# Opening loads in partition halves, 512-byte weight rows, and other operands for the warm-up matmuls in a fused state-space and gated-MLP kernel

## The chip, the cores and the metric

The kernel runs on one core of one Trainium2 chip. The metric is the device time of one execution in microseconds (us). The kernel before takes 214.58 us in the median of 4 runs (214.56 to 214.65).

## What is computed

The input x has 2048 rows of 512 values in bfloat16. It is normalised row by row, and three terms are added: x itself, a diagonal state-space layer and a gated MLP with 1792 hidden columns. Cut to what matters:

```python
xn = (x - mean(x)) / sqrt(var(x) + 1e-5)          # per row of 512
# A: h[t] = Lam_bar * h[t-1] + B_bar @ xn[t]  (512 complex states, 2048 steps)
#    yA[t] = 2 * Re(C @ h[t]) + Dskip * xn[t]
# B: yB = (silu(xn @ w1) * (xn @ w3)) @ w2         # w1, w3: 512 x 1792, w2: 1792 x 512
out = x + yA + yB
```

## The kernel before

The 2048 rows are cut into 4 blocks of 512 rows, and each block into 4 chunks of 128 rows (one row on each of the 128 partitions). The 1792 hidden columns are 14 tiles of 128 (f = 0 to 13). The engines' orders are written out by hand: an instruction goes to its engine's queue in the order in which the Python code emits it, and a small list of background tasks (`Filler`) puts VectorE work between the matmul groups.

For block 0 the start is special, and it is what the change touches.

- **Loads (L136 to L143).** The four row chunks of block 0 are loaded by one DMA each, chunks 0 and 2 from SyncE's queue (SP), chunks 1 and 3 from ScalarE's queue (ACT). Then come the gate weights: `load_w(a, b)` loads columns a to b of w1 from one queue and of w3 from the other. First f = 0 alone (rows of 256 bytes), then f = 1 and 2 (rows of 512 bytes). GpSimd's queue (POOL) loads three small parameter rows.
- **`bulk_loads` (L144 to L155).** A one-column VectorE copy into `w1_sb` (L145), which reads the statistics of chunk 1, stands ahead of it; the next load overwrites that column, so SP has to wait for the copy. Then SP issues the weights of f = 3 to 7, the next block of x, the transposing loads of B and C, the other weights.
- **Warm-up (L162 to L170).** VectorE fills a tile `warm` with zeros, and `keep_busy(9, 512)` runs nine matmuls of 512 columns on it, whose result is not used.
- **Normalisation of a chunk.** `ln_stats` (L189, L190) gives mean and variance on VectorE, `ln_first_rstd` (L203, L204) gives 1/sqrt by a logarithm and an exponential on ScalarE, `ln_apply` (L194) normalises on VectorE. `ln_first_transpose` turns the chunk by four TensorE transposes into PSUM (L209), called T0 to T3 below, and a ScalarE copy (L210) brings it to `xnT`. The pool of these PSUM tiles (`ps_y`) has two buffers, and the warm-up's output tile holds one of them.
- **Quarters (L466 to L469).** `quarter(cl, f)` multiplies chunk cl with the w1 and the w3 tile of f: 8 matmuls of 128 columns at L442. There are 12 of them, q(0,0) to q(3,2). The six PSUM tiles that they fill are then evacuated by ScalarE (L451 with Silu, L452), after `preload_act_table_set("silu_and_others")` at L500.
- From f = 3 on, block 0 goes on with matmuls of 512 columns at L442, then the state-space input (`bu`, L370), the rest of f, and the other blocks; y is formed at L546 and L552, and L557 and L558 finish and store it.

The order on TensorE at the start is: nine dummies, T0, 8 dummies of 128 columns, T1, q(0,0), q(1,0), T2, a small transpose of the parameters (L270), q(0,1), q(0,2), q(1,1), q(1,2), T3, then the six quarters of chunks 2 and 3, then f = 3.

Of the kernel before, what the change touches and what calls it, by code (L numbers as in the profile page):

```python
# [12 lines left out]
ACT = mybir.ActivationFunctionType  # L13

FP32 = DT.float32
BF16 = DT.bfloat16
P = 128
# [34 lines left out]
def kernel(  # L52
# [17 lines left out]
    nc = tc.nc  # L70
# [3 lines left out]
    CPB = 4  # L74
    TBLK = CPB * P
# [6 lines left out]
    FIRST = 3  # L82
    MID = 8
# [3 lines left out]
    xv = A_x[0].rearrange("(c p) d -> p c d", p=P)  # L87
# [3 lines left out]
    const = ctx.enter_context(tc.tile_pool(name="const", bufs=1))  # L91
# [13 lines left out]
    w1_sb = const.tile([P, NDT, F], BF16, name="w1_sb")  # L105
# [23 lines left out]
    def load_w(f0, f1, eng1=nc.sync, eng3=nc.sync):  # L129
        eng1.dma_start(out=w1_sb[:, :, f0:f1], in_=w1v[:, :, f0:f1])  # L130
        eng3.dma_start(out=w3_sb[:, :, f0:f1], in_=w3v[:, :, f0:f1])
# [1 line left out]
    def load_x(b):  # L133
        nc.sync.dma_start(out=x_blk[b], in_=xv[:, b * CPB:(b + 1) * CPB, :])

    for c in range(CPB):  # L136
        eng = nc.sync if c % 2 == 0 else nc.scalar
        eng.dma_start(out=x_blk[0][:, c, :], in_=xv[:, c, :])
    load_w(0, P, nc.sync, nc.scalar)
    load_w(P, FIRST * P, nc.sync, nc.scalar)  # L140
    for i, src in enumerate((A_log_dt, A_Lambda_re, A_Lambda_im)):
        nc.gpsimd.dma_start(out=par_rows[i * NPT:(i + 1) * NPT, :], in_=src.rearrange("(t p) -> t p", p=P))

    def bulk_loads():  # L144
        nc.vector.tensor_copy(out=w1_sb[:, 0, FIRST * P:FIRST * P + 1], in_=mv_all[:, 1, 0:1])  # L145
        load_w(FIRST * P, MID * P)
        load_x(1)
        nc.sync.dma_start_transpose(out=bt_re, in_=A_B_re)
        nc.sync.dma_start_transpose(out=bt_im, in_=A_B_im)
        load_w(MID * P, 11 * P)  # L150
        load_w(11 * P, F)
        nc.sync.dma_start_transpose(out=ct_re, in_=A_C_re)
        nc.sync.dma_start_transpose(out=ct_im, in_=A_C_im)
        nc.sync.dma_start(out=w2_sb, in_=B_w2.rearrange("(t p) d -> p t d", p=P))
        nc.sync.dma_start(out=dskip_row, in_=A_Dskip.partition_broadcast(P))  # L155
# [3 lines left out]
        load_x(3)  # L159


    warm = const.tile([P, TBLK], BF16, name="warm")  # L162
    nc.vector.memset(warm, 0.0)
    wps = ps_y.tile([P, TBLK], FP32, name="y_ps")

    def keep_busy(n, cols):
        for _ in range(n):
            nc.tensor.matmul(out=wps[:, 0:cols], lhsT=warm[:, 0:P], rhs=warm[:, 0:cols], start=True, stop=True)

    keep_busy(NWARM, TBLK)  # L170
    nc.scalar.preload_act_table_set("natural_log_exp_and_others")
# [15 lines left out]
    def ln_stats(b, cl):  # L187
        stats = lnp.tile([P, 6], FP32, name="stats", bufs=4)
        nc.vector.bn_stats(out=stats, in_=x_blk[b][:, cl, :])  # L189
        nc.vector.bn_aggr(out=mv_all[:, b * CPB + cl, :], in_=stats)  # L190

    def ln_apply(b, cl):
        c = b * CPB + cl
        nc.vector.tensor_scalar(out=xn_blk[b][:, cl, :], in0=x_blk[b][:, cl, :], scalar1=mv_all[:, c, 0:1],  # L194
                                scalar2=rstd_all[:, c:c + 1], op0=ALU.subtract, op1=ALU.mult)
# [5 lines left out]
    def ln_first_rstd(cl):  # L201
        lnv = lnp.tile([P, 1], FP32, name="lnv")
        nc.scalar.activation(out=lnv, in_=mv_all[:, cl, 1:2], func=ACT.Ln, bias=eps_t, scale=1.0)  # L203
        nc.scalar.activation(out=rstd_all[:, cl:cl + 1], in_=lnv, func=ACT.Exp, scale=-0.5)  # L204

    def ln_first_transpose(cl):
        pxt = ps_y.tile([P, NDT, P], BF16, name="y_ps")
        for dt in range(NDT):
            nc.tensor.transpose(out=pxt[:, dt, :], in_=xn_blk[0][:, cl, dt * P:(dt + 1) * P], identity=ident)  # L209
        return lambda: nc.scalar.activation(out=xnT_blk[0][:, :, cl * P:(cl + 1) * P], in_=pxt, func=ACT.Copy)  # L210
# [47 lines left out]
    kr = const.tile([P, NPT], FP32, name="kr")  # L258
# [16 lines left out]
        nc.scalar.activation(out=dtv, in_=par[:, 0:NPT], func=ACT.Exp)  # L275
        gp.tensor_tensor(out=kr, in0=dtv, in1=lre, op=ALU.mult)

    def params_rho():
        nc.scalar.activation(out=rho, in_=kr, func=ACT.Exp)
        gp.tensor_tensor(out=turn, in0=dtv, in1=lim, op=ALU.mult)  # L280
        gp.tensor_scalar(out=turn, in0=turn, scalar1=1.0 / TWO_PI, scalar2=None, op0=ALU.mult)
        gp.tensor_scalar(out=fr, in0=turn, scalar1=MAGIC, scalar2=None, op0=ALU.add)
        gp.tensor_scalar(out=fr, in0=fr, scalar1=-MAGIC, scalar2=None, op0=ALU.add)
        gp.tensor_tensor(out=fr, in0=turn, in1=fr, op=ALU.subtract)
        gp.tensor_scalar(out=t0, in0=turn, scalar1=0.25, scalar2=None, op0=ALU.add)
        gp.tensor_scalar(out=ab, in0=t0, scalar1=MAGIC, scalar2=None, op0=ALU.add)
        gp.tensor_scalar(out=ab, in0=ab, scalar1=-MAGIC, scalar2=None, op0=ALU.add)
        gp.tensor_tensor(out=ab, in0=t0, in1=ab, op=ALU.subtract)
        gp.tensor_tensor(out=den, in0=lre, in1=lre, op=ALU.mult)
        gp.tensor_tensor(out=t0, in0=lim, in1=lim, op=ALU.mult)  # L290
        gp.tensor_tensor(out=den, in0=den, in1=t0, op=ALU.add)
# [143 lines left out]
    def glu(b):  # L435
        hg_blk[b] = hgp.tile([P, NFT, TBLK], BF16, name="hgT")
        xnT, hgT = xnT_blk[b], hg_blk[b]
        pend = []

        def mms(ps, w, f, tsl):  # L440
            for dt in range(NDT):
                nc.tensor.matmul(out=ps[:, tsl], lhsT=w[:, dt, f * P:(f + 1) * P], rhs=xnT[:, dt, tsl],  # L442
                                 start=(dt == 0), stop=(dt == NDT - 1))

        pair = []

        def evac(f, g_ps, u_ps):
            if f % 2 == 0:
                pair[:] = [glup.tile([P, 2, TBLK], BF16, name="g16"), glup.tile([P, 2, TBLK], BF16, name="u16")]
            g16, u16 = pair  # L450
            nc.scalar.activation(out=g16[:, f % 2, :], in_=g_ps, func=ACT.Silu)  # L451
            nc.scalar.activation(out=u16[:, f % 2, :], in_=u_ps, func=ACT.Copy)  # L452
            if f % 2 == 1:
                pend.append((f, g16, u16))

        def gate():
            f, g16, u16 = pend.pop(0)
            nc.vector.tensor_tensor(out=hgT[:, f - 1:f + 1, :], in0=g16, in1=u16, op=ALU.mult)  # L458

        f0 = 0  # L460
        if b == 0:
            f0 = FIRST
            tiles = [(ps_gu if i < 4 else ps_bu).tile([P, TBLK], FP32, name="gu_ps" if i < 4 else "bu_ps")
                     for i in range(2 * FIRST)]

            def quarter(cl, f):  # L466
                tsl = slice(cl * P, (cl + 1) * P)
                mms(tiles[2 * f], w1_sb, f, tsl)
                mms(tiles[2 * f + 1], w3_sb, f, tsl)  # L469

            ln_stats(0, 0)
            ln_first_rstd(0)
            ln_stats(0, 1)
            ln_first_rstd(1)
            bulk_loads()
            ln_apply(0, 0)
            ln_first_transpose(0)()
            keep_busy(8, P)
            ln_stats(0, 2)
            ln_first_rstd(2)  # L480
            ln_apply(0, 1)
            ln_first_transpose(1)()
            quarter(0, 0)
            ln_stats(0, 3)
            ln_first_rstd(3)
            ln_apply(0, 2)
            ln_apply(0, 3)
            quarter(1, 0)
            ln_first_transpose(2)()
            pps = params_transpose()  # L490
            params_dt(pps)
            params_rho()
            table_angles(0)
            table_angles(1)
            for f in (1, 2):
                quarter(0, f)
            for f in (1, 2):
                quarter(1, f)
            ln_first_transpose(3)()
            nc.scalar.preload_act_table_set("silu_and_others")  # L500
            for cl in (2, 3):
                for f in range(FIRST):
                    quarter(cl, f)
            evac(0, tiles[0], tiles[1])
            evac(1, tiles[2], tiles[3])
            evac(2, tiles[4], tiles[5])
            gate()
            bg.fill(2.0)
        for f in range(f0, NFT):
            if b == 0 and f == MID:  # L510
                ssm_tasks(0)
                bu(0)
            g_ps = ps_gu.tile([P, TBLK], FP32, name="gu_ps")
            mms(g_ps, w1_sb, f, slice(0, TBLK))
            u_ps = ps_gu.tile([P, TBLK], FP32, name="gu_ps")
            mms(u_ps, w3_sb, f, slice(0, TBLK))
            evac(f, g_ps, u_ps)
            if b == 0 and f == FIRST:
                sin_step((0, 0))
            elif b > 0 or f != MID - 1:  # L520
                sin_step()
            bg.fill(1.35)
            if pend and f % 2 == 0:
                gate()
        return gate
# [132 lines left out]
```

## Time and profile before

| what | value |
|---|---|
| median of 4 runs | 214.58 us |
| the profiled execution's own time | 214.56 us |
| its span, from first to last instruction | 212.5 us |
| TensorE matmuls busy | 206.9 us (97% of the span) |
| VectorE busy | 155.7 us (73%) |
| ScalarE busy | 116.4 us (55%) |
| GpSimd busy | 24.7 us (12%) |
| first row chunk on its way (DMA, from 0.73 us) | 2.82 us |
| first transposes on TensorE | at 5.84 us |
| first quarter on TensorE | at 7.23 us |
| first matmul of f = 3 | at 13.73 us |
| last DMA issue | at 209.77 us |

How to read it: PE is TensorE's matmuls, PEld its weight loads, DVE is VectorE, ACT ScalarE, POOL GpSimd, SP SyncE. A q behind a name (SPq, ACTq) is that engine's queue issuing a DMA. All times are microseconds from the first instruction. 2.06 us of the execution's own time lie outside the span. A line such as `xn<-x_blk` names the tile written and the tile read; `x4` is the number of instructions merged; what stands in square brackets is the engine's idle time before and what ended it.

### The profile page before, as it was taken

What the parts mean: (1) busy time and instruction counts of PE and PEld (TensorE: products, weight loads), DVE (VectorE), ACT (ScalarE), POOL (GpSimd) and SP (SyncE); (2) the same over time, 40 slices, a digit from 0 to 9 for tenths busy, and PEclk for the clock granted to TensorE, in tenths of its full rate; (3) what the DMA queues carried; (4) which work ended last, traced back from release to release, by engine and by line L of the source; (5) the groups of instructions that cost most, each with busy time, mean ns of one, the idle gap of its engine ahead of it and who ended that gap; (6) DMA issues with size and microseconds to landing.
All of it is one profiled execution on the core that took longest, in us unless ns stands there. A gap on an engine that the chain in (4) does not pass through costs nothing.

```text
span 212.5 us, 2774 instructions
## 1 busy us (share of the span) xinstructions
PE 206.9 (97%) x1056; PEld 98.7 (46%) x1056; DVE 155.7 (73%) x186; ACT 116.4 (55%) x219; POOL 24.7 (12%) x50
## 2 busy tenths in 40 slices
PE   7899999999999999999999999999999999999993
PEld 2774444444444444444444444444444444444463
DVE  3599799999937969899999897828999981121111
ACT  3689897699866864066666786036667620000000
POOL 7170279300000030000000012000000000000000
PEclk9999999999999999999999999999999999999999
DMA  4999999700000003500000001510000000100100
GB/s 139 336 245 261 252 282 222 222 0 0 3 0 0 0 0 77 96 27 0 0 0 5 0 0 25 123 52 0 2 0 0 3 0 2 48 25 29 48 25 26
DMA packets 26797, 13.68 MB, mean 64 GB/s; under 512 B 16544, under 2 KB 26784, under 8 KB 26784
## 3 DMA queue, kind: packets, MB, share of 16 engines
q1 hardware_dynamic: 25200, 12.78, 25.0%
q10 hardware_dynamic: 1488, 0.72, 1.2%
q8 instruction: 8, 0.13, 0.3%
q14 instruction: 5, 0.04, 0.1%
q0 software_dynamic: 96, 0.00, 0.0%
HBM read 7.74 MB, written 2.10 MB: 46 GB/s over the span
## 4 chain that ended last, share of the span: by engine, by line
PE 94%; ACT 1%; DMA 1%; DVE 1%; issue 0%
PE gu_ps L442 45%; PE y_ps L546 23%; PE y_ps L552 13%; PE bu_ps L370 12%; DMA x_blk<-in_A_x_dram 1%; PE bu_ps L442 1%; PE y_ps L209 1%; DVE stats L189 1%; ACT xnT L210 1%; ACT u L372 1%; ACT tabe L337 0%; DVE o L557 0%; DVE mv_all L190 0%; DVE xn L194 0%; DVE w_sb L145 0%
## 5 line engine op out<-in xcount | busy, mean ns | idle before, releaser
L442 PE MATMUL gu_ps<-xnT,w_sb 128*128 128x512 bf16 (+1 forms) x488 | 96.7, 358 | 0.2 <-ACT xnT L210 0.2
L442 PEld LDWEIGHTS <-w_sb 128*128 128x128 bf16 x520 | 46.9, 98 | 50.3 <-issue 0.4
L546 PE MATMUL y_ps<-w_sb,hgT 128*128 128x512 bf16 (+1 forms) x238 | 50.2, 366 | 0.0
L452 ACT ACTIVATE u<-gu_ps 128x512 bf16<-128x512 f32 x55 | 33.3, 606 | 11.4 <-PE gu_ps L442 10.8
L451 ACT ACTIVATE g<-gu_ps 128x512 bf16<-128x512 f32 x55 | 33.2, 603 | 9.4 <-PE gu_ps L442 9.4
L557 DVE TENSOR_TENSOR o<-y_ps,xn 128x512 bf16<-128x512 f32 (+1 forms) x17 | 11.2, 657 | 36.0 <-PE y_ps L552 36.0
L546 PEld LDWEIGHTS <-hgT 128*128 128x128 bf16 x238 | 23.3, 98 | 25.3
L372 ACT ACTIVATE u<-bu_ps 128x512 bf16<-128x512 f32 x32 | 19.1, 597 | 24.2 <-PE bu_ps L370 24.2
L406 DVE TENSOR_TENSOR_SCAN u<-rho,h,u 128x512 bf16<-128x512 f32 x24 | 29.5, 1270 | 0.2
L458 DVE TENSOR_TENSOR hgT<-g,u 128x1024 bf16<-128x1024 bf16 x28 | 19.0, 682 | 5.7 <-ACT u L452 5.7
L552 PEld LDWEIGHTS <-h 128*128 128x128 bf16 x136 | 13.3, 98 | 14.3
L552 PE MATMUL y_ps<-ct_re,h 128*128 128x512 bf16 (+1 forms) x68 | 16.6, 366 | 0.0
L552 PE MATMUL y_ps<-ct_im,h 128*128 128x512 bf16 (+1 forms) x68 | 16.6, 366 | 0.0
L370 PE MATMUL bu_ps<-xnT,bt_re 128*128 128x512 bf16 x64 | 16.4, 379 | 0.1
L370 PE MATMUL bu_ps<-xnT,bt_im 128*128 128x512 bf16 x64 | 16.4, 379 | 0.0
L393 DVE TENSOR_TENSOR p<-u,tabe 128x2048 bf16<-128x2048 bf16 x8 | 9.8, 1221 | 3.5 <-ACT u L372 3.4
L242 POOL TENSOR_SCALAR acc<-acc 128x4 f32<-128x4 f32 x2 | 1.0, 500 | 80.1 <-ACT xn L241 80.1
L411 DVE TENSOR_TENSOR p<-u,tabe 128x2048 bf16<-128x2048 bf16 x8 | 9.8, 1223 | 0.2
L418 DVE TENSOR_TENSOR h<-h,p 128x2048 bf16<-128x2048 bf16 x8 | 9.8, 1223 | 0.2
L396 DVE TENSOR_TENSOR u<-u,tabe 128x2048 bf16<-128x2048 bf16 x8 | 9.8, 1223 | 0.2
L400 DVE TENSOR_TENSOR u<-u,p 128x2048 bf16<-128x2048 bf16 x8 | 9.8, 1225 | 0.1
L370 PEld LDWEIGHTS <-bt_re 128*128 128x128 bf16 x64 | 6.2, 98 | 7.8 <-issue 0.3
(91 smaller groups left out, 137.1 us busy)
## 6 DMA issues: line engine op xcount, KB each, us to landing
out_dram<-o SPq DMA_DIRECT2D x15, 128.0 KB, 1.7
w_sb<-in_B_w_dram SPq DMA_DIRECT2D x1, 1792.0 KB, 9.6
x_blk<-in_A_x_dram SPq DMA_DIRECT2D x3, 512.0 KB, 4.9
w_sb<-in_B_w_dram SPq DMA_DIRECT2D x4, 384.0 KB, 4.9
w_sb<-in_B_w_dram SPq DMA_DIRECT2D x2, 640.0 KB, 5.3
x_blk<-in_A_x_dram ACTq DMA_DIRECT2D x2, 128.0 KB, 3.1
x_blk<-in_A_x_dram SPq DMA_DIRECT2D x2, 128.0 KB, 2.9
w_sb<-in_B_w_dram SPq DMA_DIRECT2D x1, 256.0 KB, 6.0
```

What stands on the lines that cost most here:

```text
L370: nc.tensor.matmul(out=ps, lhsT=bt[:, dt, pt * P:(pt + 1) * P], rhs=xnT_blk[b][:, dt, :], start=(dt == 0), stop=(dt == NDT - 1))
L372: nc.scalar.activation(out=u[:, j, ri, :], in_=ps, func=ACT.Copy)
L393: nc.vector.tensor_tensor(out=st["p"], in0=st["g"], in1=tabe[:, psl, 1:3, :], op=ALU.mult)
L396: nc.vector.tensor_tensor(out=st["g"], in0=st["g"], in1=tabe[:, psl, 0:1, :].to_broadcast(FULL), op=ALU.mult)
L406: nc.vector.tensor_tensor_scan(out=v, data0=rho[:, pt:pt + 1].to_broadcast([P, TBLK]), data1=v, initial=init, op0=ALU.mult, op1=ALU.add)
L442: nc.tensor.matmul(out=ps[:, tsl], lhsT=w[:, dt, f * P:(f + 1) * P], rhs=xnT[:, dt, tsl], start=(dt == 0), stop=(dt == NDT - 1))
L451: nc.scalar.activation(out=g16[:, f % 2, :], in_=g_ps, func=ACT.Silu)
L452: nc.scalar.activation(out=u16[:, f % 2, :], in_=u_ps, func=ACT.Copy)
L458: nc.vector.tensor_tensor(out=hgT[:, f - 1:f + 1, :], in0=g16, in1=u16, op=ALU.mult)
L546: nc.tensor.matmul(out=tiles[cl][:, dsl], lhsT=hg_blk[b][:, f, cl * P:(cl + 1) * P], rhs=w2_sb[:, f, dsl], start=(f == 0), stop=False)
L552: nc.tensor.matmul(out=tiles[cl][:, dsl], lhsT=h_blk[b][:, pt, ri, cl * P:(cl + 1) * P], rhs=ct[:, pt, dsl], start=False, stop=(ri == 1 an ...
L557: nc.vector.tensor_tensor(out=o[:, dsl], in0=tiles[cl][:, dsl], in1=xn_blk[b][:, cl, dsl], op=ALU.add)
```

## The change

```diff
-    for c in range(CPB):
-        eng = nc.sync if c % 2 == 0 else nc.scalar
-        eng.dma_start(out=x_blk[0][:, c, :], in_=xv[:, c, :])
-    load_w(0, P, nc.sync, nc.scalar)
-    load_w(P, FIRST * P, nc.sync, nc.scalar)
+    for c in range(2):
+        nc.sync.dma_start(out=x_blk[0][0:P // 2, c, :], in_=xv[0:P // 2, c, :])
+        nc.scalar.dma_start(out=x_blk[0][P // 2:P, c, :], in_=xv[P // 2:P, c, :])
+    load_w(0, 2 * P, nc.sync, nc.scalar)
+    for c in range(2, CPB):
+        nc.sync.dma_start(out=x_blk[0][:, c, :], in_=xv[:, c, :])
+    load_w(2 * P, 4 * P)
...
     def bulk_loads():
-        nc.vector.tensor_copy(out=w1_sb[:, 0, FIRST * P:FIRST * P + 1], in_=mv_all[:, 1, 0:1])
-        load_w(FIRST * P, MID * P)
+        nc.scalar.activation(out=w1_sb[:, 0, 4 * P:4 * P + 1], in_=rstd_all[:, 0:1], func=ACT.Copy)
+        load_w(4 * P, MID * P)
...
-    warm = const.tile([P, TBLK], BF16, name="warm")
-    nc.vector.memset(warm, 0.0)
+    ones = nc.const_aps.tensor(1.0, (P, TBLK), BF16)
...
-            nc.tensor.matmul(out=wps[:, 0:cols], lhsT=warm[:, 0:P], rhs=warm[:, 0:cols], start=True, stop=True)
+            nc.tensor.matmul(out=wps[:, 0:cols], lhsT=ones[:, 0:P], rhs=ones[:, 0:cols], start=True, stop=True)
...
-    def params_rho():
-        nc.scalar.activation(out=rho, in_=kr, func=ACT.Exp)
+    def params_turn():
...
             ln_stats(0, 0)
             ln_first_rstd(0)
+            bulk_loads()
             ln_stats(0, 1)
             ln_first_rstd(1)
-            bulk_loads()
             ln_apply(0, 0)
             ln_first_transpose(0)()
-            keep_busy(8, P)
+            keep_busy(4, P)
+            ln_apply(0, 1)
+            ln_first_transpose(1)()
             ln_stats(0, 2)
             ln_first_rstd(2)
-            ln_apply(0, 1)
-            ln_first_transpose(1)()
-            quarter(0, 0)
             ln_stats(0, 3)
             ln_first_rstd(3)
             ln_apply(0, 2)
             ln_apply(0, 3)
-            quarter(1, 0)
-            ln_first_transpose(2)()
+            quarter(0, 0)
+            quarter(0, 1)
             pps = params_transpose()
             params_dt(pps)
-            params_rho()
+            params_turn()
             table_angles(0)
             table_angles(1)
-            for f in (1, 2):
-                quarter(0, f)
-            for f in (1, 2):
-                quarter(1, f)
+            quarter(1, 0)
+            quarter(1, 1)
+            quarter(0, 2)
+            quarter(1, 2)
+            ln_first_transpose(2)()
             ln_first_transpose(3)()
+            nc.scalar.activation(out=rho, in_=kr, func=ACT.Exp)
             nc.scalar.preload_act_table_set("silu_and_others")
```

Each of chunks 0 and 1 is now loaded by two DMAs, partitions 0 to 63 from SP's queue and 64 to 127 from ACT's. The weights of f = 0 and 1 follow as one pair of DMAs with rows of 512 bytes (SP and ACT), then on SP alone chunks 2 and 3 and the weights of f = 2 and 3, again with rows of 512 bytes. The one-column write ahead of the bulk loads moves from VectorE to ScalarE and reads chunk 0's 1/sqrt. The dummies read a constant one that the framework writes with a GpSimd memset at the very start (L642 in the profile), through an access pattern of stride 0; the `warm` tile and its memset go. On TensorE the order becomes: nine dummies, T0, 4 dummies, T1, q(0,0), q(0,1), parameters, q(1,0), q(1,1), q(0,2), q(1,2), T2, T3, then the six quarters of chunks 2 and 3. The exponential that gives `rho` moves from behind `kr` to just ahead of the table load.

## The prediction

> **What bounds the kernel now.** I read the page first. TensorE is busy for 97% of the span, and the chain of waits is nearly all TensorE:
>
> ```profile
> PE 206.9 (97%) x1056; PEld 98.7 (46%) x1056; DVE 155.7 (73%) x186; ACT 116.4 (55%) x219; POOL 24.7 (12%) x50
> PE 94%; ACT 1%; DMA 1%; DVE 1%; issue 0%
> ```
>
> So an edit counts only if it moves the time from which TensorE works without a break, or adds a break. The chain in order of time shows where that is:
>
> ```profile
> 0.73 2.82 DMA x_blk<-in_A_x_dram
> 3.57 0.70 DVE stats L189
> ...
> 5.09 0.19 DVE mv_all L190
> ...
> 5.31 0.16 DVE w_sb L145
> 5.47 0.33 DVE xn L194
> ...
> 5.84 0.50 PE y_ps L209 x4
> ...
> 6.36 0.61 ACT xnT L210
> ...
> 7.01 0.40 PE y_ps L209 x4
> ...
> 13.82 8.71 PE gu_ps L442 x40
> ```
>
> Up to 7 us the chain is chunk 0's load, its statistics, T0, its copy, T1; from 13.8 us on it is almost only matmuls (the largest break after that is about 0.1 us near 27.7). The first f = 3 matmul at 13.73 us in TensorE's timeline is therefore my gauge: the end moves by as much as it does. Everything this change touches lies ahead of it, and useful TensorE work is neither added nor removed.
>
> TensorE's and ScalarE's timelines give the steps:
>
> ```profile
> 1.18 4.02 PE L168 MATMUL y_ps<-warm 128*128 128x512 bf16 x9 [1.18 <-DVE warm L163]
> 5.84 0.48 PE L209 MATMUL y_ps<-ident,xn 128*128 128x128 bf16 x4 [0.64 <-DVE xn L194]
> 7.01 0.38 PE L209 MATMUL y_ps<-ident,xn 128*128 128x128 bf16 x4 [0.24 <-ACT xnT L210]
> 8.08 0.61 PE L442 MATMUL gu_ps<-xnT,w_sb 128*128 128x128 bf16 x8 [0.24 <-ACT xnT L210]
> ```
> ```profile
> 11.17 0.60 ACT L210 ACTIVATE xnT<-y_ps 128x512 bf16<-128x512 bf16 x1 [0.80 <-PE y_ps L209]
> 11.79 1.28 ACT L500 ACT_TABLE_LOAD   x1
> ```
>
> T1 waited for ScalarE's copy of T0, not for its own chunk: the copy ends at 6.96, T1 starts at 7.01. That stays so, since the order T0, copy, dummies, T1 and the two buffers stay. A quarter takes 0.446 us (q(1,0) at 8.08, T2 at 8.53).
>
> **The change, part by part.** Let S be the start of chunk 0's statistics, 3.57 now.
>
> 1. *Chunk halves (S).* Now SP's queue carries all of chunk 0 beside chunk 1 on ACT's. DMA counts up to 2.53 us and up to 2.74 us, where each packet of 1 KB is one row:
>
> ```profile
> q1 hardware_dynamic: 65, 0.07, 10.0%
> ```
> ```profile
> q10 hardware_dynamic: 63, 0.06, 6.7%
> ```
>
> q1 is SP's queue and q10 ACT's. SP's first 64 rows are under way at 2.53, its 128 at about 2.93 (139 counted with completion packets), and the chunk is usable at 3.55, 0.6 later. ACT's first 64 are under way at 2.74, so both halves of chunk 0 would be usable at about 3.34 if ACT's queue starts as late as now (2.34). It may start earlier, as it now stands behind 128 rows of SP's and then behind 64: ACT's store at the end has its first packet 1.2 us after its issue at 209.77, which here would be 1.9 and give about 3.0. Ends 3.0 and 3.55; I take 3.25, so S = 3.27. **Gain 0.30.** Chunk 1 is needed 0.83 us after S and landed at 3.73 now; it hides.
>
> The Trainium skill, "DMA: Bandwidth & Descriptors", section "Rules for kernel authors", speaks against this: two transfers to disjoint partition halves aren't worth it, since both spread over the same 16 engines and serialise. By it this term would be 0 and the time about 214.5. The packet counts say that the halves needn't be faster in sum, only ahead of chunk 1.
>
> 2. *The gate copy leaves VectorE.* Now `ln_apply` of chunk 0 starts at 5.38, behind the cast at 5.31, which waits for chunk 1's L190 (5.09 + 0.18). Without the cast it follows that L190 by 0.10, as 4.30 to 4.40 shows: S + 1.62 instead of S + 1.81; 1/sqrt is ready at S + 1.54. **Gain 0.19.** On ScalarE the copy costs 0.2 to 0.3 (rows L203, L204) just ahead of chunk 1's logarithm and delays it by at most 0.1; T1 waits for chunk 0's copy some 0.4 later than for chunk 1, which hides it. SP's bulk issues start near 5.1 instead of 5.50, behind the first loads in the same queue. Their first users come past 15 us, and x1 and the transposes later still.
>
> 3. *T0 to q(0,0).* From 5.38 to 5.84 are 0.46, to the copy 0.52, copy and T1's start 0.65, T1 0.22. T0 comes 0.5 earlier, and the clock matters: the nine dummies are 0.43 apart for 512 columns, later matmuls of that size 0.22 (40 in 8.79), and T0's 0.48 against T1's 0.38 is the change-over. All slow, T0 to copy would be 0.64; at T1's pace 0.42. I take 0.56: **loss 0.04**. So q(0,0) starts at Q = S + 1.62 + 0.46 + 0.56 + 0.65 + 0.22 = S + 3.51 = 6.78 (now 7.23 = S + 3.66).
>
> 4. *Dummies on ones.* They wait for the preamble (about 0.8) instead of the memset (1.18) and end near 4.7 at 0.427 each. No row shows a stride-0 operand; below I bound it by 0.216 each, above by what fits until T0 at 5.35, 0.5 each, which costs nothing; every 0.1 more costs 0.45 by nine of them. I take 0.427: nothing. The idle gap before T0 stays near 0.65. Four dummies fewer and VectorE's memset lie in waits.
>
> The Trainium skill, "TensorE: Matmul & The Clock Gate", Part 1, puts the rise of the clock after a window of about 3.4 us of sustained work. By that rule the earlier dummies could have T0 on the full clock, and the sum would be 214.1. The trace shows 4 us of dummies all at 0.43.
>
> 5. *The order of the quarters.* Now, from q(0,0) to f = 3 (6.50 us): 12 quarters 5.35, T2 and T3 0.44, parameters 0.20, a wait for chunk 1's copy 0.40 (7.68 to 8.08), a wait for the first evacuation 0.08. Afterwards the 0.40 goes, as q(0,1) and the parameters stand there. But T2 and T3 now stand directly ahead of q(2,0), which needs T2's copy: 0.42 from T2's start (T3 at 10.75, copy at 11.17), 0.60, 0.05, that is 1.07, of which T2 and T3 fill 0.45. **A new wait of 0.62.** `rho` adds 0.2 on ScalarE ahead of the table load, yet copy, `rho`, load (1.28) and first evacuation end 3.6 after T2's start and TensorE comes at 3.75, so the 0.08 goes too. 6.50 - 0.48 + 0.62 = 6.64: **loss 0.14**.
>
> 6. *Weights.* f = 0 and 1 (512 KB) come after 256 KB of x. The same 768 KB ahead are now needed for f = 0's w3 (ACT's second last issue at 1.65 plus 5.4), landed at 7.05; by bytes alone 0.77 MB are moved near 5.5, plus 0.4 to 0.6. Ends 6.0 and 7.05, and half as many rows; I take 6.3, needed at 6.78. f = 2's come as the 9th and 10th DMA, behind 1.54 MB in all, on SP alone, which issues them at about 3.3 and 3.8. Now 1.52 MB are moved by 8.0, plus 0.4 gives 8.4; stretching the 1.28 MB that landed at 8.3 by 1.2 gives 9.6. They are needed at Q + 1.94 (w1) and Q + 2.17 (w3), 8.72 and 8.95. I take 8.5: nothing, with little room. Chunks 2 and 3 should land by 7.1; T2 at Q + 2.8 = 9.6 leaves some 0.8 for their statistics.
>
> **Sum:** -0.30 - 0.19 + 0.04 + 0.14 = -0.31. The profiled execution's 214.56 (span 212.5 and 2.06 around it) lies 0.02 under the median, so 214.25.
>
> **Rivals.**
> - *Earlier still* (0.17): ACT's queue starts sooner, S = 3.1, and T0 runs at T1's pace: 0.17 and 0.14 more, about 213.95. For it: ACT's 1.2 us at the end. Against it: slow dummies to the end.
> - *The opening is no earlier* (0.13): chunk 0's upper half, or w3 of f = 0, lands when its like lands now (3.55, 7.05). The terms without S sum to nothing: about 214.5.
> - *f = 2's weights become the wait* (0.20, the other side): q(0,2) stands on TensorE with everything behind it. Each us past 8.95 costs one us. From 9.26 the change is a loss, from 9.7 one that shows. At the 9.6 of the stretch 214.9, with a slow tail 215.4. For it: two queues became one, and the DMA share now is only 0.53 between 4 and 5 us. Against it: that stretch carries rows of 256 bytes, which go.
>
> **How the numbers follow.** The forecast has 0.50, its own range 214.05 to 214.45. A change of 0.2% is 0.43 us, about what a measurement of this kernel can tell from no change, so faster means under 214.15 and slower over 215.01. Faster: 0.17 and a quarter of the forecast's, 0.29. Slower: two thirds of the last rival, 0.13. Within: 0.58. The range runs from 213.85 to 215.0.
>
> **What would show it.** Right: statistics from 3.27, no cast, q(0,0) near 6.8, a break of 0.6 behind T3, f = 3 near 13.4. Wrong: statistics still at 3.55; a DMA as releaser of q(0,0) or q(0,2); dummies over 0.5 each, or quarters of twice 0.446 from a late clock, each costing 0.45.

## The result: 0.39% slower, and outside the range

The changed kernel takes 215.43 us in the median of 37 runs, the kernel before 214.51 in the median of 59. The ratio is 1.0039 with a 95% interval of 1.0029 to 1.0048. The forecast was 214.25 and its range ended at 215.0. One of the 37 runs (218.58 us at a granted clock of 0.992) was slow: ratios here and below are taken from fast runs alone, so they aren't the quotients of the medians beside them.

The profiled execution of the changed kernel took 215.10 us with a span of 213.0; before it was 214.56 and 212.5. Its page shows TensorE as busy as it was (206.9 before), but the chain of waits is no longer TensorE's alone:

```profile
PE 207.1 (97%) x1052; PEld 98.3 (46%) x1052; DVE 155.6 (73%) x184; ACT 116.5 (55%) x220; POOL 24.7 (12%) x50
PE 81%; DVE 7%; DMA 5%; ACT 4%; ACTq 1%; POOL 1%; issue 0%; DVEq 0%
```

TensorE's share fell by 13 points, and those of VectorE, DMA and ScalarE rose. Something after the opening now ends last. TensorE's timeline of the opening first (start, time, what; the idle time before it in brackets):

```profile
0.76 3.95 PE L169 MATMUL y_ps<-const-bfloat16-1.0 128*128 128x512 bf16 x9 [0.76 <-PEq L643]
5.28 0.40 PE L210 MATMUL y_ps<-ident,xn 128*128 128x128 bf16 x4 [0.56 <-DVE xn L195]
...
5.99 0.40 PE L210 MATMUL y_ps<-ident,xn 128*128 128x128 bf16 x4
6.36 0.38 PE L442 MATMUL gu_ps<-xnT,w_sb 128*128 128x128 bf16 x4
7.28 0.84 PE L442 MATMUL gu_ps<-xnT,w_sb 128*128 128x128 bf16 x12 [0.54 <-DMA w_sb<-in_B_w_dram]
...
10.11 0.61 PE L210 MATMUL y_ps<-ident,xn 128*128 128x128 bf16 x8
11.18 1.05 PE L442 MATMUL gu_ps<-xnT,w_sb 128*128 128x128 bf16 x16 [0.46 <-ACT xnT L211]
...
13.86 0.38 PE L442 MATMUL gu_ps<-xnT,w_sb 128*128 128x512 bf16 x1
```

T0 comes 0.56 earlier than before and q(0,0) 0.87 earlier (6.36 against 7.23). Then q(0,0) stands for half its work until w3 of f = 0 has landed, and behind T3 (T2 and T3 are the eight at 10.11) stands the new wait that the prediction worked out. f = 3 starts at 13.86, 0.13 later than before. The chain of the changed kernel between 28 and 70 us, in order of time, shows the other loss:

```profile
31.54 3.46 DVE u L406 x3
35.00 0.08 DVE hgT L458
35.08 5.12 DMA xnT<-xn
40.20 0.25 issue
40.44 24.33 PE gu_ps L442 x112
```

`xnT<-xn` is the transpose of block 1's normalised rows, four transposing DMAs, one for each chunk, that stand in SP's queue behind the load of w2 (L156) and a row of parameters, `dskip_row` (L157):

```profile
26.95 0.58 SPq L156 DMA_DIRECT2D w_sb<-in_B_w_dram  x1
27.57 1.09 SPq L157 DMA_DIRECT2D dskip_row<-in_A_Dskip_dram  x1
28.77 4.68 SPq L214 DMA_TRANSPOSE xnT<-xn  x2
```

The last transpose is issued at 35.08 and lands at 40.20; 0.24 us later TensorE goes on. In the kernel before, the same stretch of TensorE's timeline is one line without a break, and the last transpose landed at 38.93:

```profile
37.69 4.48 PE L442 MATMUL gu_ps<-xnT,w_sb 128*128 128x512 bf16 x20
```

The two changes account for the span. Later matmuls are 0.22 apart. In the changed kernel the last one before the break starts at 39.76, so the next was due at 39.98, and block 1's xnT was due 0.24 before that, at 39.74: f = 3's start plus 25.88. It landed at 40.20, so the wait is 0.46. 212.5 + 0.13 + 0.46 = 213.1, against 213.0 in the profile. Before, xnT was due at 13.73 + 25.88 = 39.61, and there were 0.68 us to spare.

### The profile page after: what moved, and what is told of

Same layout as the page of the kernel before. It is cut to its first block, busy times and chain, and to the rows that moved or that the text cites. A ratio compares the mean times of both kernels' runs of the same rounds, so it can differ in the third digit from the quotient of the medians.

```text
span 213.0 us, 2770 instructions
## 1 busy us (share of the span) xinstructions
PE 207.1 (97%) x1052; PEld 98.3 (46%) x1052; DVE 155.6 (73%) x184; ACT 116.5 (55%) x220; POOL 24.7 (12%) x50
## 4 chain that ended last, share of the span: by engine, by line
PE 81%; DVE 7%; DMA 5%; ACT 4%; ACTq 1%; POOL 1%; issue 0%; DVEq 0%
PE gu_ps L442 35%; PE y_ps L547 23%; PE y_ps L553 13%; PE bu_ps L370 10%; DMA xnT<-xn 2%; DMA w_sb<-in_B_w_dram 2%; DVE u L406 2%; ACT g L451 1%; DVE stats L190 1%; ACT u L452 1%; ACTq L138 1%; DVE xn L195 1%; ACT L501 1%; DVE u L400 1%; DVE hgT L458 1%; DVE p L393 1%
```

## The experiments

Two theories stood at first. **The queue theory** (Theory A in the texts below): the end is set by block 1's xnT, which is last in SP's queue behind w2 (1.8 MB), so the gains of the opening can't reach the end. **Its rival, the opening theory** (Theory B): the opening itself lost the time, by the wait for w3 and by T2 and T3 ahead of q(2,0). Each kernel was timed in five rounds beside the kernel before on the same chip (214.33 to 214.43 us there); ratios are to that, with 95% intervals.

### w2 behind the transposes, and T2 back in its place

`e1_w2_behind` is the changed kernel with two loads moved behind block 1's transposes:

```diff
     def bulk_loads():
...
-        nc.sync.dma_start(out=w2_sb, in_=B_w2.rearrange("(t p) d -> p t d", p=P))
-        nc.sync.dma_start(out=dskip_row, in_=A_Dskip.partition_broadcast(P))
...
     def late_loads():
+        nc.sync.dma_start(out=dskip_row, in_=A_Dskip.partition_broadcast(P))
+        nc.sync.dma_start(out=w2_sb, in_=B_w2.rearrange("(t p) d -> p t d", p=P))
         load_x(2)
```

> The changed kernel, with the loads of w2 (1792 KB) and of the Dskip row issued behind the four transposing DMAs of block 1's xnT instead of ahead of them. Theory A (xnT of block 1, last in SP's queue, lands too late for TensorE near 40 us): the wait at 40 us goes, xnT lands near 32 us, only the 0.13 us by which f = 3 starts later stays, 214.65, and the spread of the runs shrinks. Theory B (the loss lies in the first 14 us, in the late w3 of f = 0 and the wait behind T3, and varies there): 215.4, unchanged.

`e2_t2_early` is the changed kernel with T2 ahead of q(0,2); `e3_both` has both edits, and `e4_before_w2_behind` has the edit of e1 in the kernel before.

```diff
             quarter(1, 1)
+            ln_first_transpose(2)()
             quarter(0, 2)
             quarter(1, 2)
-            ln_first_transpose(2)()
```

> The changed kernel, with chunk 2's transposes T2 put back ahead of q(0,2), so that their copy runs beside q(0,2) and q(1,2). Both theories expect f = 3 to start 0.6 us earlier (13.3 instead of 13.9). Theory A: TensorE then only waits longer for xnT of block 1 near 40 us, so the time stays at 215.3 to 215.4. Theory B: the gain reaches the end, 214.8.

> The changed kernel with both edits: w2 and Dskip behind xnT of block 1, and T2 ahead of q(0,2). Theory A: only now does T2's 0.6 us reach the end, 214.05, under the kernel before. Theory B: as with T2 alone, 214.8.

> The kernel before, with w2 and Dskip behind xnT of block 1. In its profile xnT lands at 38.9 and is needed at about 39.9, so both theories expect nothing: 214.5. A gain of more than 0.2 us would say that xnT was late in many runs of the kernel before as well.

| kernel | median, us | ratio | f = 3 | xnT of block 1 landed | wait at 40 |
|---|---|---|---|---|---|
| e1, w2 behind | 214.68 | 1.0017 [0.9998, 1.0036] | 14.84 | 33.23 | none |
| e2, T2 early | 215.12 | 1.0041 [1.0020, 1.0062] | 13.02 | 39.87 | 0.97 |
| e3, both | 213.81 | 0.9986 [0.9969, 1.0004] | 13.41 | 34.22 | none |
| e4, before with w2 behind | 214.27 | 0.9997 [0.9988, 1.0006] | 13.45 | 32.7 | none |

e2 decides between the two, by its trace: its median of 215.12 lies between the 215.3 of the queue theory and the 214.8 of the other. T2's place brought f = 3 to 13.02, 0.71 earlier than in the kernel before, and the ratio is that of the changed kernel. TensorE's timeline of e2 near 40 us:

```profile
36.76 2.54 PE L442 MATMUL gu_ps<-xnT,w_sb 128*128 128x512 bf16 x11
40.11 2.10 PE L442 MATMUL gu_ps<-xnT,w_sb 128*128 128x512 bf16 x9 [0.82 <-ACT u L452]
```

All that was won in the opening, and more, is lost here: the wait is 0.97. The profile names ScalarE's evacuation as the releaser, but the restart lies 0.24 after the landing at 39.87, the same distance as in the changed kernel (40.20, 40.44). It is the same wait. And with w2 out of the way there is none, in e1 and e3. So the queue theory holds as far as it goes: the wait is real, and it is cured by a shorter queue. The opening theory is a part: T2's place brings f = 3 forward by 0.45 us in e3 and 0.84 in e2 (against 13.86), but this reaches the end only where the queue lets it through. In the kernel before, where nothing waits, the shorter queue alone is worth nothing that can be told (e4).

e1 showed something that neither theory had. Its median met the queue theory's 214.65, but its spread did not shrink: seven executions lie between 213.87 and 214.81 and five between 215.08 and 215.74. The profiled one is among the five, with f = 3 only at 14.84. Its TensorE timeline:

```profile
5.52 0.61 PE L210 MATMUL y_ps<-ident,xn 128*128 128x128 bf16 x4 [0.76 <-DVE xn L195]
...
6.99 1.91 PE L442 MATMUL gu_ps<-xnT,w_sb 128*128 128x128 bf16 x16
```

Sixteen quarter matmuls in 1.91 us, where the changed kernel's profile has 1.07 for as many. The distance between two starts is 0.107 until 9.6 us, then 0.056. The view by windows gives a granted clock of 1.00 all the while. The list of granted clocks kept in the packed trace shows more: it has no entry ahead of 9.71 us in this execution and begins there at full speed, while in the changed kernel's profile it begins at 4.53. The distances change where the list begins. That is **cause C** (Theory C): with nine dummies that now start at 0.76 instead of 1.18 and end near 4.7 instead of 5.2, the clock may come up 4 to 5 us late.

### More dummies, and whole chunks

```diff
-    NWARM = 9
+    NWARM = 11
```

`e8_after_warm11` is the changed kernel with this edit alone, `e5_both_warm11` is e3 with it, and `e6_both_warm11_whole` is e5 with chunk 0 whole on SP's queue and chunk 1 whole on ACT's. `e7_before_ones` is the kernel before with the dummies on the constant ones and nothing else.

```diff
-        nc.sync.dma_start(out=x_blk[0][0:P // 2, c, :], in_=xv[0:P // 2, c, :])
-        nc.scalar.dma_start(out=x_blk[0][P // 2:P, c, :], in_=xv[P // 2:P, c, :])
+        (nc.sync if c == 0 else nc.scalar).dma_start(out=x_blk[0][:, c, :], in_=xv[:, c, :])
```

> The changed kernel with w2 and Dskip behind xnT of block 1, T2 ahead of q(0,2), and eleven dummies of 512 columns instead of nine. In the profile of the run without T2's move the quarters ran at half speed until 9.7 us; the nine dummies now end at 4.7 and leave TensorE idle until T0 at 5.5. Theory C (the idle gap lets the clock come up late in some executions): eleven dummies close the gap, the times above 214.8 (3 of 12 with nine dummies) go, the median is 213.6. Rival (the late clock is chance, or comes from the ones as operands): as many runs above 214.8 as with nine, median 213.8.

> As the run with eleven dummies, and chunks 0 and 1 loaded whole again, chunk 0 from SP's queue and chunk 1 from ACT's. If halving is worth what the prediction gave it, chunk 0's statistics start 0.3 us later and the time is 213.9. If the longer issues of the half loads (0.58 to 0.87 us each against 0.39 to 0.46) give it back through later weights, 213.6, no change.

> The kernel before with one part of the change: the dummies read the constant ones, so they start at 0.8 instead of 1.2 us and end 0.4 earlier, and the idle gap ahead of T0 grows from 0.6 to about 1.0 us. Theory C: in more of the runs the clock comes up late, runs of 215 to 216 appear and the median rises to 214.6 or more. Rival (the operands and the start of the dummies don't matter, as the prediction had it): 214.4, the spread of the kernel before.

> The changed kernel with eleven dummies instead of nine and nothing else. Theory A with C: xnT of block 1 still ends the wait near 40 us, which hides a late clock in part, so only a part goes: 215.0. If the late clock were the whole loss: 214.5. If the clock were nothing: 215.4.

| kernel | median, us | ratio | f = 3 | xnT of block 1 landed |
|---|---|---|---|---|
| e5, both edits and eleven dummies | 213.74 | 0.9971 [0.9960, 0.9983] | 13.11 | 34.78 |
| e6, e5 with whole chunks | 213.62 | 0.9973 [0.9962, 0.9984] | 12.78 | 32.80 |
| e7, before with ones | 214.29 | 1.0005 [0.9992, 1.0018] | 13.41 | 39.42 |
| e8, the change with eleven dummies | 214.43 | 1.0006 [0.9992, 1.0020] | 13.88 | 38.51 |

Without the late wait and with the clock up, the new order is worth something: **e6 has the lowest median, 213.62 us, with e5 at 213.74 within its noise, and both beat both kernels.** Its opening on TensorE has no wait for a weight and none behind T3:

```profile
5.51 0.40 PE L209 MATMUL y_ps<-ident,xn 128*128 128x128 bf16 x4 [0.89 <-DVE xn L194]
...
6.59 1.05 PE L441 MATMUL gu_ps<-xnT,w_sb 128*128 128x128 bf16 x16
...
12.78 1.46 PE L441 MATMUL gu_ps<-xnT,w_sb 128*128 128x512 bf16 x5
```

The halves bring the first statistics to 3.28 in e5 against 3.45 in e6, and yet e6 is not slower. Queue times suggest why. This is ACT's queue in the changed kernel (start, time, what):

```profile
0.73 1.48 ACTq L138 DMA_DIRECT2D x_blk<-in_A_x_dram  x2
2.24 0.60 ACTq L131 DMA_DIRECT2D w_sb<-in_B_w_dram  x1
```

and this in the kernel before:

```profile
0.72 0.90 ACTq L138 DMA_DIRECT2D x_blk<-in_A_x_dram  x2
1.65 1.08 ACTq L131 DMA_DIRECT2D w_sb<-in_B_w_dram  x2
```

Two issues of 64 rows take 1.48, two of 128 rows 0.90. In e6 only one chunk stands ahead on each queue, the weights of f = 0 and 1 are issued at 1.15 and 1.18 and land by 5.34, and nothing waits for them. Chunk 2's load is issued at 1.64 and lands at 5.90; in e5, behind two halves and a weight load, it is issued at 2.88 and lands at 6.82, and there T2 waits for that chunk's rows:

```profile
8.91 0.40 PE L210 MATMUL y_ps<-ident,xn 128*128 128x128 bf16 x4 [0.21 <-DVE xn L195]
```

e8 shows something that the clock can't explain. Its median, 214.43, met the 214.5 that was expected if the late clock was the whole loss, but by another way: f = 3 starts no earlier, and the two dummies removed the wait at 40 us, as xnT landed at 38.51, 1.7 earlier than in the changed kernel. e7 missed Theory C's 214.6 and met its rival's 214.4: the constant ones by themselves cost nothing in the median. But 2 of its 11 executions lie at 215.26 and 215.52, where none of the 24 of the kernel before beside it is over 214.88.

### Two by two

On another chip I ran the changed kernel again, with eleven dummies, with w2 behind, and with both.

> The changed kernel itself, once more, on the same chip as the three runs beside it, so that the two suspects can be priced against each other: nine or eleven dummies, and w2 with Dskip ahead of or behind xnT of block 1. Both theories: 215.2 to 215.5, above the kernel before.

> The changed kernel with eleven dummies, w2 still ahead of xnT. Theory C (the late clock is most of the loss): 214.6, since f = 3 starts at 13.9 on the full clock. Theory A (xnT of block 1 is most of it): 215.0 or more, with a wait of TensorE near 40 us in the profile.

> The changed kernel with nine dummies and w2 and Dskip behind xnT. Theory A: 214.6, with only a few runs above 215. Theory C: 215.0 or more, the runs above 215 as many as in the changed kernel.

> The changed kernel with both, eleven dummies and w2 behind xnT; the wait behind T3 stays. Both theories: nothing is left but the start of f = 3 at about 13.9, so 214.5, within 0.1 of the kernel before, and a narrow spread.

| kernel | median, us | ratio | f = 3 | xnT landed | wait |
|---|---|---|---|---|---|
| f1, the change again | 215.47 | 1.0048 [1.0034, 1.0062] | 13.59 | 41.04 | 1.57 |
| f2, eleven dummies | 214.07 | 0.9997 [0.9985, 1.0009] | 13.60 | 39.02 | none |
| f3, w2 behind | 214.26 | 1.0011 [0.9993, 1.0028] | 14.67 | 33.09 | none |
| f4, both | 214.05 | 0.9983 [0.9970, 0.9995] | 13.40 | 34.27 | none |

The two edits don't add: each takes about 1.2 to 1.4 us off the median, and both together hardly more. f2 and f4 came out some 0.5 us under the numbers expected of them, in part because f = 3 starts at 13.60 and 13.40 there and not at 13.9; what tells most is that f1's wait is gone in f2. f3's median is under both theories' numbers too, with 4 of 12 executions above 215. Near 40 us TensorE's timeline has this line in f1:

```profile
41.29 1.02 PE L442 MATMUL gu_ps<-xnT,w_sb 128*128 128x512 bf16 x4 [1.42 <-DMA xnT<-xn]
```

f1's clock was up before T0 and its f = 3 starts 0.01 from f2's, so no loss of TensorE's time in the opening explains 2.0 us between their landings. Cause C is a separate thing: f3's profiled execution again has quarters at 0.107 until 9.3 us. In the 36 executions of e1, e3 and f3 (nine dummies, no wait at 40 us) 12 lie over 1 us above the fastest of their series; in the 24 of e5, e6 and f4 (eleven dummies) none does. In the kernel before, whose nine dummies end at 5.20, it is 5 of 171.

### Where TensorE's instructions are fetched

One difference between the traces of f1 and f2 ahead of the late transposes stands out: a 16 KB DMA whose kind is "instruction" (queue q8) moves at 35.28 in f1 and at 32.76 in f2. (It isn't the only one: the first transpose is issued at 28.38 and 28.01, and w2 landed at 36.65 and 36.10.) The DMA view between 35 and 37 us lists it for the changed kernel (packets, MB, share of the 16 engines):

```profile
q1 hardware_dynamic: 831, 0.23, 212.9%
q14 instruction: 1, 0.01, 5.7%
q8 instruction: 1, 0.02, 3.6%
```

and for f2 between 32 and 34 us:

```profile
q1 hardware_dynamic: 942, 0.59, 264.6%
q14 instruction: 1, 0.01, 9.0%
q8 instruction: 1, 0.02, 3.6%
```

The page of the changed kernel counts eight such fetches in the span, one for each 130 or so of its 1052 matmuls, so q8 looks like TensorE's. **Theory D**: the change has four dummies fewer, which moves that fetch in among the transposes. Four kernels with the number of short dummies changed (`keep_busy(n, P)` behind T0) and, in g3, eleven long ones:

> The changed kernel with eight short dummies behind T0 instead of four, as many as before; nothing else differs. Theory D (where TensorE's instruction fetch falls decides; it follows the number of TensorE instructions): the fetch that falls at 35.3 to 35.9 with four goes back to about 32.8, block 1's xnT lands by 39.4, the wait near 40 us is gone, about 214.4 with a part of the executions at 215.2 to 215.8 from the late clock. Rival C (the idle stretch ahead of T0 and the clock decide): nothing changes, the wait stays, 215.4. Rival K (chance from execution to execution): a mix of both, 214.4 to 215.6 without a pattern.

> The changed kernel with six short dummies instead of four: nine long ones as in the change, but as many TensorE instructions as with eleven long and four short. Theory D: the fetch at about 32.8, no wait near 40 us, about 214.3 to 214.5. Rival C: fetch without meaning, the wait stays, 215.4.

> The changed kernel with eleven long and two short dummies: no idle stretch ahead of T0, but as many TensorE instructions as in the change. Theory D: the fetch at 35 to 36 again and the wait for xnT back, about 215.1. Rival C: as with eleven and four, no wait, 214.1.

> The kernel before with four short dummies instead of eight, nothing else. Theory D: the fetch moves from 32.8 to about 35 and block 1's xnT lands about 1 us later than at 38.9, so at about 39.9: the wait just begins, 214.4 to 214.9. Rival C: nothing, 214.4, xnT by 39.4.

| kernel (long + short dummies) | matmuls | fetch at | xnT due, landed | wait | median, ratio |
|---|---|---|---|---|---|
| before (9 + 8) | 1056 | 32.77 | 39.61, 38.93 | none | 214.51 |
| g1, the change (9 + 8) | 1056 | 32.72 | 39.72, 39.41 | none | 214.62, 1.0014 [0.9998, 1.0030] |
| g2, the change (9 + 6) | 1054 | 33.44 | 39.75, 39.40 | none | 215.02, 1.0038 [1.0026, 1.0049] |
| f2, the change (11 + 4) | 1054 | 32.76 | 39.48, 39.02 | none | 214.07, 0.9997 [0.9985, 1.0009] |
| e8, the change (11 + 4) | 1054 | 32.73 | 39.76, 38.51 | none | 214.43, 1.0006 [0.9992, 1.0020] |
| the change (9 + 4) | 1052 | 35.94 | 39.74, 40.20 | 0.46 | 215.43, 1.0039 [1.0029, 1.0048] |
| f1, the change again (9 + 4) | 1052 | 35.28 | 39.47, 41.04 | 1.57 | 215.47, 1.0048 [1.0034, 1.0062] |
| g3, the change (11 + 2) | 1052 | 36.38 | 39.70, 39.96 | 0.26 | 215.01, 1.0034 [1.0021, 1.0048] |
| g4, before (9 + 4) | 1052 | 35.43 | 39.39, 38.62 | none | 214.34, 1.0000 [0.9989, 1.0011] |

Shown: with 1052 matmuls the fetch moves at 35.3 to 36.4, with more at 32.7 to 33.4, in nine of the ten kernels with w2 and T2 in place, whether nine or eleven dummies are long. (Where w2 or T2 is moved the times are others, and again later with 1052 matmuls, 32.1 to 35.7, than with more, 29.3 to 30.1.) The tenth is e7: it has 1056 matmuls like the kernel before, and its fetch is at 29.40. So the number says which fetch is the later one and not where it falls, and why four matmuls of under 1 us in all move it by 2.7 to 3.2 us isn't known. Shown too: in the seven traces of the changed kernel with w2 and T2 in place, one execution each, there is a wait in the three with 1052 matmuls and in none of the four with more. g1 and g3 came out as D expected: g1 has nine long dummies and no wait, and g3 has the eleven long dummies of f2, two short ones fewer, and is at 215.01 where f2 was at 214.07. Chance, the rival, isn't met by g1's times alone (214.22 to 215.51), but none of g3's six executions is under 214.82.

How the fetch delays the transposes is read from where the landings fall and wasn't tested by itself. In the kernel before, the first transpose lands 0.49 after the transfer ahead of it in the queue (36.43 to 36.92). In the changed kernel this distance is 2.62 (36.18 to 38.80), in f1 2.65, in g3 1.98. In each the first transpose ends 0.7 to 1.1 after the last instruction fetch has ended: q14's at 36.26, which took 1.81, in the changed kernel; q14's at 34.51, which took 4.21, in f1; q8's at 36.38, which took 1.13, in g3. In f2 q14's fetch ends at 36.65, and the transpose lands 1.0 after it, at 37.65, early enough. Such a distance doesn't bring a wait by itself: g1 and g2 have 1.0 too, and in the kernel before the second transpose lands 1.0 after a fetch of q14. In e2 and e7 no fetch ends among the transposes, and they land 0.45 to 0.55 apart.

Three rows speak against D as the whole story. e2 has a wait of 0.97 with no fetch among its transposes: w2 landed there only at 37.51, and xnT was due 0.84 earlier than in the changed kernel. g4 has the late fetch and no wait: its transposes were queued earlier (w2 landed at 34.80, in the changed kernel at 35.77), and it met D's expectation for the fetch and missed it for xnT, 38.62 instead of 39.9. So the late fetch cost something only where the queue had no room left. And g2 missed D's 214.3 to 214.5: its median stayed at 215.02, though its profiled execution (214.56, the fastest of its six) has no wait: which of the two causes its other executions had isn't known, as one execution of each kernel has a trace. g1 and g2 also don't leave the opening as it was, since T1 waits for ScalarE's copy again there (0.22 and 0.34).

## Why the prediction was wrong

**The step that failed is the gauge**: "the end moves by as much as" the first f = 3 matmul does, from the chain, which named no wait after 13.8 us. A chain shows what ended last; it doesn't show by how little the next thing missed ending last. Block 1's xnT had 0.68 us to spare, and that could be read before: the last landing at 38.93 against the first matmul that uses it. With the wait as a second term the gauge holds in every profiled run: span = 212.5 + (f = 3's start - 13.73) + wait, to within 0.15. For e2 this gives 212.8 (profile 212.7), for f1 213.9 (213.8), for e6 211.6 (211.6), for e1 213.6 (213.5). The rivals had the same blind spot: all three lay in the opening.

What ate the 0.68 us: not the issue times. The first transpose of block 1 was issued at 28.77 instead of 28.00 (block 1's x at 7.25 instead of 6.46), but the transfer ahead of the transposes, `dskip_row`, landed at 36.18, and at 36.43 before: the queue was no later up to there. The loss lies behind it. The first transpose landed 2.62 after that row instead of 0.49, the next three made up 0.6 of this, and xnT landed 1.3 later. f1 lost the same there (37.06 to 39.71). That the instruction fetches did this is the reading above; why they hold up the transposes stays open. "Their first users come past 15 us, and x1 and the transposes later still" treated SP's queue as free because its early entries had time. Its last entries hadn't.

By the prediction's own steps:

1. *Chunk halves.* Right: 3.20, expected 3.27.
2. *The gate copy.* Right: no cast, `xn` at 4.84, which is S + 1.64 (expected 1.62).
3. *T0 to q(0,0).* Too slow by 0.35 (1.08 instead of 1.43). T0 ran at T1's pace in this execution, and T1 didn't wait for ScalarE's copy, "that stays so" in the prediction: it started at 5.99, 0.28 into the copy. In the program T1 waits on TensorE's own work here, that is on the dummies' buffer, while with six or eight short dummies it waits on ScalarE's copy, so in these kernels the number of dummies decides which of the two buffers it gets.
4. *Dummies on ones.* 0.427 apart, as expected, and not free: they end at 4.7 instead of 5.2, which leaves TensorE idle for longer ahead of T0 (0.76 and 0.78 in e1 and f3), and the late clock came more often. The text priced that at 0.45 a quarter and gave it no chance; in e1 and f3 it cost about 1 us in some of the executions. e7's 2 of 11 may be the same in the kernel before.
5. *The order of the quarters.* Right to 0.01: T2 at 10.11, q(2,0) at 11.18, which is 1.07.
6. *Weights.* Wrong in size: w3 of f = 0 landed at 7.23, past the upper bound of 7.05, and q(0,0) stood 0.70 between its halves (four matmuls of 0.056 from 6.36 are over at 6.58, and it goes on at 7.28). The bound took over ACT's old issue time of 1.65. It was 2.24, as the two halves ahead took 0.58 longer to issue; 2.24 and 5.0 are 7.24. In f1, the same kernel, it landed at 6.67, and q(0,0) lost only 0.1. f = 2's weights, the rival on the other side, were in time in this execution; g2 waited 0.32 for them and f2 0.18.

The opening was thus 13.86 against a forecast of 13.42: 0.42 won by q(0,0) (0.07 of it in S), 0.70 lost for w3, and 0.16 in small breaks ahead of T2. The late wait adds 0.46 in the profile. The median lies 0.33 above the profiled execution. How it splits isn't known, as each kernel has one trace: f1 had a wait of 1.57, neither of the two profiles had the late clock, and some of the other executions may have. With w2 behind the transposes, which takes the wait away and leaves the late clock in, the median fell by 0.75 (to e1) and 1.2 (f1 to f3), and the ratio by 0.0022 and 0.0037, which is 0.5 and 0.8 us; so the wait is about half of the loss, or more.

On the halves the Trainium skill, "DMA: Bandwidth & Descriptors", "Rules for kernel authors", had advised one whole transfer. The landings don't bear out that nothing is won: the first statistics came 0.37 earlier. The times don't speak against the advice, with e5 at 213.74 and e6 at 213.62: what the halves win at the first chunk goes again in both queues, where they held chunk 2's load and f = 1's weights back.

On the clock the Trainium skill, "TensorE: Matmul & The Clock Gate", Part 1, says that the window of about 3.4 us runs freely and doesn't begin with the kernel. The traces agree: e6 is at the fast pace from the dummy at 3.58, f2 from 3.65, e5 only from 4.03, though their dummies start at the same 0.76. The list of granted clocks in the packed traces fits too. Its first stretch, at full speed, begins where the pace changes, at 3.44 to 9.71 us, and lasts 204.80, 208.21 or 211.63 us: the steps are 3.41. In all 18 traces the stretch of 3.41 us just ahead of the rise holds at most 0.74 us without a matmul, and each earlier stretch of the same length, which didn't raise the clock, at least 0.76. In e1 the one from 2.88 to 6.29 holds the idle 0.76 ahead of T0, and the rise is at 9.71, one stretch later. So the late clock would be a matter of where the window happens to lie and of how long TensorE stands idle in it. No run here sets either by itself, the ends of matmuls are modelled, and 0.74 and 0.76 lie close, so this stays a reading.

## What to carry to other kernels

Before counting an edit of the opening as won at the end, look for the next thing that ends late: for each later group of transfers, its last landing against its first use, and what stands ahead of it in its queue. A chain with no wait in it says nothing about slack. And when a kernel gains or loses "free" dummy work, look at what goes with the number of instructions and with the time they cover, here an instruction fetch and the clock; together they cost more than the 0.33 us that the change was meant to win.

## What the runs showed of the hardware

- Issuing a DMA of 64 rows held its queue for longer than one of 128 rows, though it moves half as much: 0.55 to 0.87 us against 0.39 to 0.50 in the runs above.
- Instruction fetches share the DMA engines with the kernel's transfers (the DMA views at 35 to 37 and 32 to 34 us), and some took 1.8 to 4.2 us for 8 KB where others took 0.3 to 0.7. Four matmuls of 128 columns at 5 us went with a fetch at 33 us moved by 2.7 (before and g4) and 3.2 us (g1 and the change), one trace each.
- The clock's rise moved by up to 6.3 us between executions of these kernels (3.4 to 9.7 us), while the view by windows gave a granted clock of 1.00 throughout.
